# Seven block products for the gate projection in two more token groups, with the work beside them placed anew

## The chip, the cores and the metric

The kernel runs on one core of a Trainium2 chip. The metric is the device time of one execution in microseconds. An execution of the kernel before takes 316.2 to 318.2 us in 27 fast runs (median 316.66 in the last session), so a difference under about 0.5 us is read from the profiles, not from the times. All runs shown here were in the fast state.

In lines of the profile, PE is TensorE and PEld its weight loads, DVE is VectorE, ACT is ScalarE, POOL is GpSimd and SP is SyncE; POOL and SP issue the DMAs spoken of here. L593 is line 593 of that run's kernel, so line numbers differ between the kernel before and the changed one. A bank is one of the eight parts of PSUM, in which TensorE adds up its results.

## The reference, cut to what matters

```python
def _attn_ref(q, k, v):                      # 8 batches, 8 heads, 576 positions, 64 features
    q_p, k_p = phi(q, cos, sin), phi(k, cos, sin)     # phi(x) = [relu(x)*cos, relu(x)*sin]
    kv  = einsum('bhsf,bhsd->bhfd', k_p, v);  z = sum(k_p, axis=2)
    num = einsum('bhsf,bhfd->bhsd', q_p, kv)
    den = einsum('bhsf,bhf->bhs', q_p, z) + 1e-06
    return num / den

def _moe_ref(x, w_gate, w_val, w_out):       # x: 4608 tokens x 512;  d_ff = 1536
    g = x @ w_gate
    return (g * sigmoid(g) * (x @ w_val)) @ w_out
```

## The kernel before

The 4608 tokens go through in nine groups (0 to 8) of 512. A group has a **gate stage** (gate and value projections, twelve blocks of 128 features, one slot each) and an **output stage** (four slots). While TensorE works on group g, the attention of the tokens of group g+1 is done in gaps: `at(slot, function)` puts a piece of it after a slot. Sixteen slots make one group. A batch has 576 positions, so batches and groups don't coincide: from batch 4 on, the q of batch b is prepared while TensorE works on group b-2, so that of batch 7 in group 5.

In groups 7 and 8 the gate projection is formed from seven block products in place of eight, with additions between them on VectorE and copies on ScalarE:

```python
GATE = (7, 8)
...
rel  = ctx.enter_context(tc.tile_pool(name="rel", bufs=1))     # r_q: the weighted q of one batch
rawq = ctx.enter_context(tc.tile_pool(name="rawq", bufs=3))
...
def product(to, u, a, x, first):                               # one block product: 4 matmuls of 256 columns
    for i in range(2):
        for c in range(KH):
            nc.tensor.matmul(out=to[:, i], lhsT=a[:, c, 2 * u + i], rhs=x[:, :, c], ...)

for u in range(3):
    a = bank("a", fills=True);  product(a, u, A11, B11, True)
    b = bank("b", seeded=True); nc.scalar.copy(out=b, in_=a)
    e = bank("e", fills=True);  product(e, u, W3, X3, True)
    nc.scalar.copy(out=m7, in_=e); free("e")
    V(...)                                                      # a value block: 4 matmuls of 512 columns
    product(b, u, W2, X2, False)
    c = bank("c", seeded=True)
    nc.vector.tensor_tensor(out=c, in0=m7, in1=b, op=ALU.add)   # the seeding addition
    product(a, u, A12, B21, False); silu(u, 1, 0, a); free("a")
    if u: mul(u - 1, 1, 1)
    ...
    product(c, u, A22, X4, False)                               # needs the seeding addition
```

An attention tile takes two PSUM banks and is normalised on VectorE at once. A batch's q is weighted into `r_q` on VectorE (`phi_q`) and turned by a transposing DMA on SP's queue (`qturn_dma`, L306 before, L323 after) into `phit`, which the tiles read:

```python
def a_tile2(t):
    ps = take(2)
    ... nc.tensor.matmul(out=ps[...], lhsT=phit[b][...], rhs=kv2s[b % 2][...]) ...
    x_of(t, ps)                                # den, reciprocal, product: three VectorE instructions

def load_behind(b):                            # POOL
    nc.gpsimd.tensor_copy(out=hold2, in_=phit[b - 1][0:1, :, 0, 0, 0])     # waits until phit[b-1] has landed
    load(b, "q")
    if b > 3: load_kv(b)
```

In the output stage `product` runs through the two halves outermost, and the stores of `out` are issued on SP's queue, the same on which the turns are issued.

## Time and profile before

| kernel before | |
|---|---|
| median time | 316.97 us (3 runs), 316.86 us with the three of the next session |
| span of the profiled run | 314.5 us |
| TensorE busy | 307.5 us, 98% |
| length of groups 2 to 7 (first gate matmul to the next group's) | 32.62, 32.40, 32.74, 32.39, 32.43, 30.87 us |

The lines that carry the reading are in the prediction below. The group lengths are read from TensorE's timeline: the start of a group's first gate matmul, taken from the start of the next group's. They are the tool of this study, because they repeat from run to run within a few hundredths of a microsecond, except where a DMA decides.

### The profile page before, as it was taken

Reading aid. Unit: us, or ns where it says so; the run is one execution under the profiler, and the core shown is the slowest. Engines: PE = TensorE matmul, PEld = TensorE weight load, DVE = VectorE, ACT = ScalarE, POOL = GpSimd, SP = SyncE. Lnnn points to the kernel's source line nnn. Section 1 sums busy time; section 2 is a strip of 40 time slices with the busy share of each in tenths; the row PEclk is TensorE's granted clock in tenths of the full one; section 3 lists DMA queues with packets and bytes.
Section 4 is the critical chain, followed back from the end, with each engine's and each line's share of the span. In section 5 each row is a group of like instructions: output and inputs, shape, how many; then the busy total and the mean of one; then the engine's idle time right before and its main releaser. Section 6 shows DMA issues by size and latency. Waiting matters only on the chain.

```text
span 314.5 us, 6775 instructions
## 1 busy us (share of the span) xinstructions
PE 307.5 (98%) x2696; PEld 189.7 (60%) x2696; DVE 228.2 (73%) x458; ACT 143.4 (46%) x264; POOL 36.0 (11%) x62
## 2 busy tenths in 40 slices
PE   8899999999999999999999999999999999999994
PEld 4597455455444585548654764577456866687673
DVE  7873777697678888587748786778779478946772
ACT  7554545763335346334543454335533345324530
POOL 7855102000200200030003000300000000000000
PEclk9999999999999999999999999999999999999999
DMA  7999999996897994989495979598951160014004
GB/s 268 217 198 197 206 205 138 226 133 99 143 208 114 150 145 110 148 119 196 100 153 75 200 144 154 73 192 135 164 86 35 40 145 17 20 38 98 0 2 133
DMA packets 74767, 41.07 MB, mean 131 GB/s; under 512 B 49904, under 2 KB 69872, under 8 KB 74736
## 3 DMA queue, kind: packets, MB, share of 16 engines
q1 hardware_dynamic: 51952, 22.55, 38.0%
q0 software_dynamic: 22192, 17.57, 37.2%
q10 hardware_dynamic: 592, 0.52, 0.5%
q8 instruction: 21, 0.34, 0.4%
q14 instruction: 10, 0.08, 0.1%
HBM read 37.75 MB, written 9.44 MB: 150 GB/s over the span
## 4 chain that ended last, share of the span: by engine, by line
PE 91%; DVE 5%; ACT 2%; issue 1%; ACTq 0%
PE banks L564 46%; PE banks L786 20%; PE banks L729 6%; PE banks L633 5%; PE banks L621 5%; PE banks L333 3%; PE banks L448 3%; DVE ht L638 1%; PE banks L494 1%; PE banks L430 1%; DVE v L287 1%; DVE sums L760 1%; DVE x L471 1%; PE banks L197 1%; PE banks L536 0%
## 5 line engine op out<-in xcount | busy, mean ns | idle before, releaser
L564 PE MATMUL banks<-xT,wg_sb 128*128 128x512 f16 (+2 forms) x368 | 86.6, 360 | 0.0
L564 PE MATMUL banks<-xT,wv_sb 128*128 128x512 f16 (+2 forms) x368 | 86.6, 360 | 0.0
L570 ACT ACTIVATE sg<-banks 128x512 bf16<-128x512 f32 (+2 forms) x92 | 51.5, 560 | 76.0 <-PE banks L564 74.0
L575 DVE TENSOR_TENSOR ht<-sg,banks 128x512 f16<-128x512 bf16 (+2 forms) x92 | 57.9, 637 | 29.7 <-PE banks L564 22.7
L564 PEld LDWEIGHTS <-wv_sb 128*128 128x128 f16 x368 | 35.5, 98 | 37.4
L564 PEld LDWEIGHTS <-wg_sb 128*128 128x128 f16 x368 | 33.9, 98 | 31.5 <-issue 0.2
L786 PEld LDWEIGHTS <-ht 128*128 128x128 f16 x336 | 32.5, 98 | 4.2
L786 PEld LDWEIGHTS <-sums 128*128 128x128 f16 x252 | 24.5, 98 | 4.2 <-issue 0.8
L633 PE MATMUL banks<-xT,wv_sb 128*128 128x512 f16 x96 | 24.3, 379 | 0.0
L283 DVE TENSOR_TENSOR r_q<-raw_q,tab 128x1152 bf16<-128x1152 bf16 x24 | 17.6, 754 | 7.4 <-ACT raw_q L266 7.1
L729 PE MATMUL banks<-wo_sb,ht 128*128 128x512 f16 x96 | 22.7, 379 | 0.0
L471 DVE TENSOR_TENSOR x<-banks,rec 128x512 f16<-128x512 f32 (+1 forms) x32 | 21.6, 674 | 1.3 <-PE banks L430 0.3
L786 PE MATMUL banks<-wo_sb,ht 128*128 128x256 f16 x168 | 20.6, 273 | 0.0
L287 DVE TENSOR_TENSOR v<-raw_v,tab 128x1152 bf16<-128x1152 bf16 x27 | 19.9, 751 | 0.5 <-ACT raw_v L849 0.5
L786 PE MATMUL banks<-wt_sb,sums 128*128 128x256 f16 x168 | 19.8, 273 | 0.1
L786 PE MATMUL banks<-wt_sb,ht 128*128 128x256 f16 x168 | 19.5, 273 | 0.0
L799 ACT ACTIVATE ob<-banks 128x512 f32<-128x512 f32 x14 | 8.4, 597 | 21.9 <-PE banks L786 21.9
L638 DVE TENSOR_TENSOR ht<-sg,banks 128x512 f16<-128x512 bf16 x24 | 15.5, 681 | 2.4 <-ACT sg L627 2.4
L266 ACT ACTIVATE raw_k<-raw_k 128x576 bf16<-128x576 bf16 (+1 forms) x25 | 17.1, 694 | 0.0
L998 POOL COPY hold<-phit 1x2 bf16<-1x2 bf16 x5 | 1.4, 287 | 129.3 <-DMA phit<-r_q 129.3
L760 DVE TENSOR_TENSOR sums<-ht 128x1024 f16<-128x1024 f16 (+1 forms) x28 | 15.5, 553 | 0.4
L266 ACT ACTIVATE raw_q<-raw_q 128x576 bf16<-128x576 bf16 x24 | 15.4, 675 | 0.0
(121 smaller groups left out, 334.6 us busy)
## 6 DMA issues: line engine op xcount, KB each, us to landing
out_dram<-ob SPq DMA_DIRECT2D x67, 128.0 KB, 2.5
raw_k<-in_k_dram POOLq DMA_DIRECT2D x7, 576.0 KB, 8.8
raw_q<-in_q_dram POOLq DMA_DIRECT2D x6, 576.0 KB, 6.0
raw_v<-in_v_dram POOLq DMA_DIRECT2D x6, 576.0 KB, 11.4
wo_sb<-in_moe_w_out_dram POOLq DMA_DIRECT2D x3, 512.0 KB, 12.8
wg_sb<-in_moe_w_gate_dram POOLq DMA_DIRECT2D x5, 256.0 KB, 9.4
wv_sb<-in_moe_w_val_dram POOLq DMA_DIRECT2D x5, 256.0 KB, 9.5
wo_sb<-in_v_dram SPq DMA_DIRECT2D x2, 576.0 KB, 4.0
```

Of the source, the lines that this page charges most:

```text
L266: nc.scalar.activation(out=out, in_=in_, func=AF.Relu)
L283: nc.vector.tensor_tensor(out=st[b, "q"][:, g], in0=o.unsqueeze(2).to_broadcast([P, NC, 2, D]), in1=tab, op=ALU.mult)
L287: nc.vector.tensor_tensor(out=v2s[b == 1][:, g, :, :, 0:D], in0=(first if b == 0 and g == 0 else {"v": raw_of(b, "v")})["v"][:, g].unsquee ...
L471: nc.vector.tensor_tensor(out=st["x", t].rearrange("p (y e d) -> p e y d", e=2, d=D)[:, :, ys], in0=ps[:, :, 0:2 * J * D1].rearrange("p e ...
L564: nc.tensor.matmul(out=st["f", tg, fc, lo][i], lhsT=(wg_sb, wv_sb)[i][:, kc, fs], rhs=xT[tg][:, ts, kc], start=(kc == 0), stop=(kc == KC - 1))
L570: nc.scalar.activation(out=sg[:, 0:n], in_=st["f", tg, fc, lo][0], func=AF.Silu, scale=DOWN)
L575: nc.vector.tensor_tensor(out=ht[:, fc, r:r + n], in0=st.pop(("s", tg, fc, lo))[:, 0:n], in1=ps[1], op=ALU.mult)
L633: nc.tensor.matmul(out=val[u, i, w], lhsT=wv_sb[:, kc, fc * P:(fc + 1) * P], rhs=xT[tg][:, :, kc], start=(kc == 0), stop=(kc == KC - 1))
L638: nc.vector.tensor_tensor(out=ht[:, fc], in0=gates[u, w][:, i], in1=val.pop((u, i, w)), op=ALU.mult)
L729: nc.tensor.matmul(out=o_ps[t], lhsT=ht[:, fc, r:r + P], rhs=wo_sb[:, fc], start=(fc == 0), stop=(fc == FC - 1))
L760: nc.vector.tensor_tensor(out=o[:, lo:hi], in0=x[:, lo:hi], in1=y[:, lo:hi], op=op)
L786: nc.tensor.matmul(out=to[i][:, 0] if len(to) == 2 else to[0][:, i], lhsT=a[:, kc, i * P:(i + 1) * P], rhs=b[:, kc], start=first and kc == ...
```

## The change

The intent is to use the seven products in groups 5 and 6 also, which frees 1.2 us of TensorE in each, and to make room on VectorE and in PSUM so that nothing waits. The core of the diff:

```diff
-    GATE = (7, 8)
+    GATE = (5, 6, 7, 8)
+    AHEAD = 5
+    WSUM = (31, 39, 47, 63)
+    ROW = {... 5: ((8, 9, 12, 12), 13, (13, 13, 14, 15), 5),        # q weighting, turn, v products, kv slot
+           6: ((6, 8, 9, 12), 13, (13, 13, 14, 15), 3),
+           7: ([4 + i // 2 for i in range(18)], 13, (12, 13, 14, 15), 3)}
+    TILES = {... 5: (2, 4, 7, 9), 6: (0, 2, 5, 7), 7: (0, 1, 5, 7), 8: (0, 3, 5, 7)}
+    LATE = dict(M=44, V=87, O=131, X=26, x=150, ...)                # estimated ends of use, for the bank choice
...
-                bs = [min((b for b in free ...), key=lambda b: (not any(...), used[b]))]
+                bs = [min((b for b in free ...), key=lambda b: used[b])]
...
+    def phi_q_part(b, c, w):                    # batch 7: eighteen pieces on ScalarE
...
+        nc.scalar.activation(out=st[b, "q"][:, :, c, w], in_=raws[b, "q"][:, :, c], func=AF.Relu,
+                             scale=csk[:, c, w:w + 1])
...
-        x_of(t, ps)
+        if later:
+            behind.append(lambda: (x_of(t, ps), give_back(("a2", t), LATE["x"]), x_turn(t)))
+        else:
+            x_of(t, ps)
...
             nc.vector.tensor_tensor(out=c, in0=m7, in1=b, op=ALU.add)
+            while behind:
+                behind.pop(0)()
...
-            for i in range(2):
-                for kc in range(HC):
+            for kc in range(HC):
+                for i in range(2):
                     nc.tensor.matmul(out=to[i][:, 0] if len(to) == 2 else to[0][:, i], ...)
...
+        queues = (nc.gpsimd, nc.gpsimd) if tg > 0 else None          # stores of groups 1 to 7
...
         nc.gpsimd.tensor_copy(out=hold2, in_=phit[b - 1][0:1, :, 0, 0, 0])
-        load(b, "q")
+        if b < AHEAD:
+            load(b, "q")
         if b > 3:
             load_kv(b)
+        if AHEAD <= b + 1 < B:
+            load(b + 1, "q")
```

Cut: half of the kv evacuation is postponed in the same way, a gate product and token sums change places, and the slot arithmetic that `ROW` and `TILES` replace.

More of the change, by code (lines that the diff above doesn't have):

```diff
@@ L51 @@
     KH = KC // 2
-    GATE = (7, 8)
+    GATE = (5, 6, 7, 8)
+    AHEAD = 5
+    WSUM = (31, 39, 47, 63)
+    ROW = {2: ((16, 16, 17, 17), 18, (20, 21, 21, 22), 8), 3: ((12, 13, 14, 15), 18, (20, 20, 21, 21), 7),
+           4: ((12, 12, 13, 14), 15, (15, 16, 17, 18), 5), 5: ((8, 9, 12, 12), 13, (13, 13, 14, 15), 5),
+           6: ((6, 8, 9, 12), 13, (13, 13, 14, 15), 3), 7: ([4 + i // 2 for i in range(18)], 13, (12, 13, 14, 15), 3)}
+    TILES = {2: (0, 9, 10, 11), 3: (5, 9, 10, 11), 4: (5, 7, 9, 11), 5: (2, 4, 7, 9), 6: (0, 2, 5, 7), 7: (0, 1, 5, 7), 8: (0, 3, 5, 7)}
+    LATE = dict(M=44, V=87, O=131, X=26, x=150, v=(190, 250, 120, 150), e=130, a=90, c=170, b=110, k=120)
     consts = ctx.enter_context(tc.tile_pool(name="consts", bufs=1))
@@ L77 @@
     loose = [False]
+    rows = [0]
     def take(n, hold=None, fills=False, seeded=False):
@@ L84, in take @@
             if n == 1:
-                bs = [min((b for b in free if filled[b] or not seeded), key=lambda b: (
-                    not any(x != b and x + 1 != b and x + 1 in free for x in free), used[b]))]
+                bs = [min((b for b in free if filled[b] or not seeded), key=lambda b: used[b])]
             else:
@@ L105, in take, with touch, give_back @@
         return banks[:, b0] if n == 1 else banks[:, b0:b0 + n]
-    def touch(r):
+    def touch(r, late=1):
         now[0] += 1
+        if loose[0]:
+            for x in r:
+                used[x] = rows[0] + late
+            return
         for x in r:
             used[x] = now[0]
-    def give_back(hold):
-        touch(held.pop(hold))
+    def give_back(hold, late=1):
+        touch(held.pop(hold), late)
     raws = {}
@@ L284, in phi_q @@
                                 in1=tab, op=ALU.mult)
+    def phi_q_part(b, c, w):
+        if (b, "q") not in st:
+            st[b, "q"] = rel.tile([P, G, NC, 2, D], BF16, name="r_q")
+        nc.scalar.activation(out=st[b, "q"][:, :, c, w], in_=raws[b, "q"][:, :, c], func=AF.Relu,
+                             scale=csk[:, c, w:w + 1])
     def vmul(b, g):
@@ L347, in kv_out @@
                     in_=ps[hs, e, js.start * 2 * D1:js.stop * 2 * D1].rearrange("p (y x) -> p y x", x=D1))
+    behind = []
     kv2s = [consts.tile([P, 2, J, 2, D1], BF16, name=f"kv2_{j}") for j in range(2)]
@@ L353, in kv_out2, with part @@
         ps = st[b, "kvps"][:, :, 0:4 * J * D1 // 2].rearrange("p e (j w x) -> p e j w x", j=J, w=2)
-        for w, eng in enumerate((nc.scalar.copy, nc.vector.tensor_copy)):
+        def part(w, eng):
             for i in range(2):
                 eng(out=kv2s[b % 2][w * D:(w + 1) * D, :, :, i], in_=ps[i * D:(i + 1) * D, :, :, w])
+        part(0, nc.scalar.copy)
+        if b - 1 in GATE:
+            behind.append(lambda: (part(1, nc.vector.tensor_copy), kv_free(b)))
+        else:
+            part(1, nc.vector.tensor_copy)
     def kv_free(b):
-        give_back(("kv", b))
+        give_back(("kv", b), LATE["k"])
     def kv_first(j, lo=0, hi=NC):
@@ L435, in a_tile, with a_tile2 @@
                 )
-    def a_tile2(t):
+    def a_tile2(t, later=False):
         (b0, c0), (b1, c1) = (divmod(2 * t + r, NC) for r in range(2))
-        ps = take(2)
+        ps = take(2, ("a2", t))
+        rows[0] += LATE["X"]
         if b0 == b1:
@@ L452, in a_tile2 @@
                     )
-        x_of(t, ps)
+        if later:
+            behind.append(lambda: (x_of(t, ps), give_back(("a2", t), LATE["x"]), x_turn(t)))
+        else:
+            x_of(t, ps)
+            give_back(("a2", t), LATE["x"])
     def x_den(t, ps, ys=slice(0, 4)):
@@ L613, in bank, with free @@
             return take(1, ("g", tg, nm), **kw).rearrange("p (i x) -> p i x", i=2)
-        def free(nm):
-            give_back(("g", tg, nm))
+        def free(nm, late):
+            give_back(("g", tg, nm), late)
         def product(to, u, a, x, first):
+            rows[0] += LATE["M"]
             for i in range(2):
@@ L631, in V @@
             val[u, i, w] = take(1, ("v", tg, fc), fills=True)
+            rows[0] += LATE["V"]
             for kc in range(KC):
@@ L638, in mul @@
             nc.vector.tensor_tensor(out=ht[:, fc], in0=gates[u, w][:, i], in1=val.pop((u, i, w)), op=ALU.mult)
-            give_back(("v", tg, fc))
+            give_back(("v", tg, fc), LATE["v"][2 * w + i])
         def done():
@@ L653, in ffn_by_quarters @@
             nc.scalar.copy(out=m7, in_=e)
-            free("e")
+            free("e", LATE["e"])
             V(*((u - 1, 1, 1) if u else (u, 0, 0)))
@@ L659, in ffn_by_quarters @@
             nc.vector.tensor_tensor(out=c, in0=m7, in1=b, op=ALU.add)
+            while behind:
+                behind.pop(0)()
             product(a, u, A12, B21, False)
             silu(u, 1, 0, a)
-            free("a")
-            if u:
-                mul(u - 1, 1, 1)
+            free("a", LATE["a"])
             V(u, 0, 0) if u else V(u, 1, 0)
@@ L668, in ffn_by_quarters @@
             nc.vector.tensor_tensor(out=m7, in0=m7, in1=b, op=ALU.add)
+            while behind:
+                behind.pop(0)()
             silu(u, 0, 1, m7)
+            if u:
+                mul(u - 1, 1, 1)
             product(c, u, A22, X4, False)
             silu(u, 0, 0, c)
-            free("c")
+            free("c", LATE["c"])
             V(u, 1, 0) if u else V(u, 0, 1)
@@ L675, in ffn_by_quarters @@
             if u == 2:
-                for n in (1, 2):
-                    token_sum(n, 0, 4)
+                token_sum(1, 0, 4)
             mul(u, 0, 0)
@@ L683, in ffn_by_quarters @@
             silu(u, 1, 1, b)
-            free("b")
+            free("b", LATE["b"])
             if u:
@@ L687, in ffn_by_quarters @@
             mul(u, 0, 1)
+            if u == 2:
+                token_sum(2, 0, 4)
             if u:
                 done()
-                token_sum(*((3, 0, 4) if u == 1 else (4, 0, 4)))
+            if u == 1:
+                token_sum(3, 0, 4)
         V(2, 1, 1)
@@ L720, in store_two, with ffn_out @@
                 in_=obs[t // 2][e * SH:(e + 1) * SH, :, cols])
-    def ffn_out(t, f0=0, f1=None):
+    def ffn_out(t, f0=0, f1=None, queues=None):
         f1 = FC if f1 is None else f1
@@ L738, in ffn_out @@
             nc.vector.tensor_single_scalar(out=ob_of(t), in_=ps, scalar=DOWN, op=ALU.mult)
-        store(t)
+        store(t, queues=queues)
     aq = ht.rearrange("p (i w) (h t) -> p w h i t", w=2, h=2)
@@ L783, in product @@
         def product(to, a, b, first):
-            for i in range(2):
-                for kc in range(HC):
+            rows[0] += LATE["O"]
+            for kc in range(HC):
+                for i in range(2):
                     nc.tensor.matmul(out=to[i][:, 0] if len(to) == 2 else to[0][:, i],
@@ L816, in out_by_quarters @@
             nc.vector.scalar_tensor_tensor(out=o_, in0=x_, scalar=UP, in1=p_, op0=ALU.mult, op1=ALU.add)
-        token_sum(4, 4, 6)
+        token_sum(4, 0 if tg in GATE else 4, 6)
         slot_of(0)
@@ L836, in out_by_quarters @@
             for t in (t0 + 2, t0 + 3):
-                store(t)
+                store(t, queues=queues)
         slot_of(2)
@@ L842, in out_by_quarters @@
         for t in (t0, t0 + 1):
-            store(t, *((slice(HD, d_model), (nc.sync, nc.scalar)) if last else ()))
+            store(t, *((slice(HD, d_model), (nc.sync, nc.scalar)) if last else (slice(0, d_model), queues)))
         slot_of(3)
@@ L1013 @@
     for n in range(4):
-        at(SLOTS * (1 + n * (GATE[0] - 1) // 4) + FC + 3, lambda n=n: gate_weight_sum(n))
+        at(WSUM[n], lambda n=n: gate_weight_sum(n))
     for tg in GATE:
@@ L1019 @@
         s0 = SLOTS * (b - 1)
+        p0 = s0 - SLOTS
         keng = "dve" if b == 2 else "act"
-        steps = [lambda b=b, g=g: phi_q(b, g) for g in range(G)]
-        steps += [lambda b=b, g=g: (relu_k(b, g, g + 1, keng), vmul(b, g)) for g in range(G)]
-        if b == 2:
-            fs, tq = [s0 + i for i in (0, 0, 1, 1, 4, 5, 5, 6)], (s0 + 2, s0 + 2)
-        else:
-            p0 = s0 - SLOTS
-            fs, tq = [p0 + 12, p0 + 12] + [p0 + 11 + i for i in range(2, 8)], (p0 + 15, p0 + 16)
-            if b == 3:
-                fs, tq = [p0 + 12 + i for i in range(4)] + [s0 + 4, s0 + 4, s0 + 5, s0 + 5], (s0 + 2, s0 + 2)
-            at(p0 + 3 if b < 5 else p0 + 1, lambda b=b: load_behind(b))
@@ L1031 @@
-        tk = (s0 + 4, s0 + {2: 8, 3: 7}.get(b, 5))
-        for s, f in zip(fs, steps):
-            at(s, f)
-        for e in range(2):
-            at(tq[e], lambda b=b, e=e: qturn_dma(b, e))
-        at(tk[-1], lambda b=b: kv_mm(b), lambda b=b: kv_out2(b))
-        at(tk[-1] + 1, lambda b=b: kv_free(b))
-    for t in range(2 * OUT, NTG * OUT):
-        tg, i = divmod(t, OUT)
-        s = SLOTS * (tg - 1) + (5 if tg > 2 else 4) + 2 * i
-        if t == 2 * OUT:
-            at(s, a_(t, 0))
-            at(s + 1, a_(t, 1), turn(t))
-        elif tg == 2:
-            at((9, 10, 11)[i - 1] + SLOTS, lambda t=t: a_tile2(t), turn(t))
-            if i == 2:
-                at(11 + SLOTS, load_3)
-        else:
-            if t in (13, 14, 15):
-                s = SLOTS * 2 + t - 4
-            elif tg - 1 in GATE:
-                s = SLOTS * (tg - 1) + ((1, 2, 7, 9) if tg < 6 else (1, 2, 4, 7) if tg < 8 else (1, 2, 5, 6))[i]
-            at(s, lambda t=t: a_tile2(t), turn(t))
+        phi, turned, weighed, kv_slot = ROW[b]
@@ new lines @@
+        if b > 2:
+            at(p0 + (3 if b < 5 else 1), lambda b=b: load_behind(b))
+        if len(phi) > G:
+            for i, s in enumerate(phi):
+                at(p0 + s, lambda b=b, i=i: phi_q_part(b, *divmod(i, 2)))
+        else:
+            for g, s in enumerate(phi):
+                at(p0 + s, lambda b=b, g=g: phi_q(b, g))
+        for g, s in enumerate(weighed):
+            at(p0 + s, lambda b=b, g=g: (relu_k(b, g, g + 1, keng), vmul(b, g)))
+        for e in range(2):
+            at(p0 + turned, lambda b=b, e=e: qturn_dma(b, e))
@@ new lines @@
+        at(s0 + kv_slot, lambda b=b: kv_mm(b), lambda b=b: kv_out2(b))
+        if b - 1 not in GATE:
+            at(s0 + kv_slot + 1, lambda b=b: kv_free(b))
+    at(SLOTS + 4, a_(8, 0))
+    at(SLOTS + 5, a_(8, 1), turn(8))
+    for tg in range(2, NTG):
+        for i in range(tg == 2, OUT):
+            t, s = tg * OUT + i, TILES[tg][i]
+            later = tg - 1 in GATE and s in (0, 1, 3, 4, 7, 8)
+            at(SLOTS * (tg - 1) + s, lambda t=t, later=later: (a_tile2(t, later), None if later else x_turn(t)))
+            if t == 10:
+                at(SLOTS * (tg - 1) + s, load_3)
@@ L1056 @@
         if tg in GATE:
-            loose[0] = True
+            if not loose[0]:
+                loose[0] = True
+                rows[0] = max(used) + 1
             ffn_by_quarters(tg, lambda i: slot(s0 + i))
@@ L1067 @@
         for i in range(OUT):
-            ffn_out(tg * OUT + i)
+            ffn_out(tg * OUT + i, queues=(nc.gpsimd, nc.gpsimd))
             weight_sum(i)
```

## The prediction

> **What bounds the kernel now.** I read the page's busy shares first, then the chain of waits, then a table of busy time by stage, then the groups of instructions by shape.
>
> The page of the kernel before, busy time and the chain that ended last by engine:
> ```profile
> PE 307.5 (98%) x2696; PEld 189.7 (60%) x2696; DVE 228.2 (73%) x458; ACT 143.4 (46%) x264; POOL 36.0 (11%) x62
> ...
> PE 91%; DVE 5%; ACT 2%; issue 1%; ACTq 0%
> ```
> The reader is to see that TensorE is nearly always occupied and carries 91% of the chain. So there are two sources of gain: fewer columns streamed by TensorE, and its stalls. The median time is 316.97 us over a span of 314.5 us; I keep these 2.5 us as a constant.
>
> Busy time by stretch, in order group 6 whole, group 7's gate stage, its output stage, group 8's gate stage and its output stage (columns: stretch, length, PE busy, weight loads, DVE, ACT, POOL, clock, DMA share, GB/s):
> ```profile
> 217.83:250.26 32.43, 32.43 (x295) 19.69 (x293) 23.13 (x45) 12.27 (x22) 0.00 (x0) 1.00 0.49 86
> ...
> 250.26:271.71 21.45, 21.02 (x167) 13.93 (x165) 17.59 (x35) 9.90 (x18) 0.00 (x0) 1.00 0.34 75
> 271.71:281.13 9.42, 9.34 (x86) 8.14 (x85) 5.36 (x11) 2.36 (x4) 0.00 (x0) 1.00 0.00 1
> 281.13:300.66 19.53, 19.53 (x134) 12.91 (x133) 13.81 (x23) 9.76 (x18) 0.00 (x0) 1.00 0.24 55
> 300.66:310.01 9.35, 9.31 (x84) 7.87 (x82) 5.35 (x13) 2.42 (x5) 0.00 (x0) 1.00 0.19 48
> ```
> Groups 7 and 8 already form the gate by seven block products. Group 8's gate stage takes 19.53 us and group 7's 21.45 us. Group 7 alone also does four attention tiles, 0.26 us each in the chain: 1.04 us. The other 21.45 - 19.53 - 1.04 = **0.88 us is stall**. The chain names where:
> ```profile
> 255.73 0.27 PE banks L448 x8
> 256.02 0.18 DVE den L458
> 256.22 0.21 DVE rec L467
> 256.46 0.70 DVE x L471
> 257.20 0.60 PE banks L621 x4
> ...
> 263.70 0.35 PE banks L448 x8
> 264.07 1.28 DVE ht L638 x2
> 265.46 0.21 DVE rec L467
> 265.70 0.63 DVE x L471
> 266.33 0.57 issue
> 266.91 0.70 DVE banks L659
> 267.65 0.61 PE banks L621 x4
> ```
> The reader is to see an attention tile (L448) followed at once by its normalisation on VectorE (L458, L467, L471), and TensorE's next block product (L621) starting only after that: once because the tile's PSUM bank is handed to the next product, once because the addition that seeds a block's accumulator (L659) stands behind that normalisation in VectorE's order.
>
> The rows by shape that I take durations from:
> ```profile
> L564 PE MATMUL banks<-xT,wg_sb 128*128 128x512 f16 x312 | 80.1, 379 | 0.0
> ...
> L471 DVE TENSOR_TENSOR x<-banks,rec 128x512 f16<-128x512 f32 x30 | 20.7, 691 | 1.0
> ...
> L283 DVE TENSOR_TENSOR r_q<-raw_q,tab 128x1152 bf16<-128x1152 bf16 x24 | 17.6, 754 | 7.4 <-ACT raw_q L266 7.1
> ...
> L266 ACT ACTIVATE raw_q<-raw_q 128x576 bf16<-128x576 bf16 x24 | 15.4, 675 | 0.0
> ```
> A matmul's 379 ns is latency; its rate comes from the chain: eight of 512 columns in 1.73 us there (0.216 each), eight of 256 in 0.87 us (0.109 each).
>
> **What the Trainium skill says.** "TensorE: Matmul & The Clock Gate", Wait — 56ns, not 53.3ns?: a warm matmul takes N / 2.4 GHz plus about 2.5 ns, so 215.7 ns at 512 columns and an estimated 109.2 ns at 256. The trace agrees (0.216 and 0.109), so halving the width costs almost nothing. "VectorE: DVE Perf Modes", The TRN2 errata: an fp32 addition takes (N+151)/0.96 ns, 691 ns at 512; the trace has 695 for L659 and 686 for L668. "ScalarE: Activation LUTs", What ACT_TABLE_LOAD costs: 186 ns + 0.833 ns per element, 93 ns more for a per-partition scale, neighbours overlapping by 93 ns. For the new 256-element pieces I estimate 186 + 213 + 93 = 492 ns, 0.4 us back to back; L504, of 260 elements with such a scale, shows 475. "SBUF — State Buffer", Who interferes with whom: DMA does not contend with compute engines, but descriptors written by GpSimd can be held up by VectorE. That matters for the moved stores; no trace yet shows it.
>
> **The change part by part.**
> 1. Gate of groups 5 and 6 by seven products. Before: 12 blocks x 4 = 48 matmuls of 512 columns, 48 x 0.216 = 10.37 us a group. After: 3 x 7 x 4 = 84 of 256, 84 x 0.109 = 9.14 us. Saved 1.22 us, twice: **-2.44 us**, all on the path, as TensorE is the path there. The instruction order confirms 72 more matmuls.
> 2. Its price on VectorE: four differences of 0.42 (1.67), three additions of 0.695 and three of 0.686 (4.14): 5.8 us a group; on ScalarE six copies of 0.58 (3.5 us). None of it is on the path unless VectorE becomes late. In issue order group 5 then has, on VectorE: 12 gate products 8.2, four tiles 4.2, block additions 4.1, token sums 4.3, three output additions 2.1, four v products 3.0, kv copies 0.9, differences 1.7: 28.4 us. Neighbours overlap: in the group before, a like sum of 26.7 shows as 24.7 busy, a factor 0.93. So about 26.3 us against some 31.2 us of TensorE; group 6, without the v products, 23.6. In the gate stage alone about 19 of 21.8. Tight, not bound.
> 3. Room made for it: batch 7's query weighting goes from VectorE (4 x 0.754 = 3.0 us less) to ScalarE (18 x about 0.45 = 8 us, less the four dropped 0.675: about +5.4 us, to some 22 of 31 us in group 5); batches 5 and 6 are turned earlier, inside the gate stage; attention tiles move to earlier slots. Net 0 on the path.
> 4. Tile normalisations and half of the kv evacuation wait until after the seeding addition, a last gate product moves behind the m7 addition, and a token sum leaves its place ahead of them. PSUM banks go by estimated end of use instead of by last touch. Both aim at group 7's 0.88 us. I give back two thirds: **-0.6 us**.
> 5. Chunks outermost in the output stage: the four chunks whose sums are early come first for both halves, so the last sums have 4 x 0.109 = 0.44 us more. The chain shows gaps of 0.03 us in seven output stages and about 0.07 in group 7: **-0.2 us**.
> 6. Weight sums sooner: the same four 0.95 us instructions, elsewhere: 0. Stores of groups 1 to 7 go through POOL instead of SP: 56 issues of about 0.75 us are 42 us of an engine that is busy 36 of 314; 0 on the path.
> 7. New stalls in groups 5 and 6, which do what group 7 does plus kv (and, in group 5, v) work: by the same reasoning 0.88 x 1/3 = 0.3, plus 0.05 for the kv copies: **+0.7 us** for both.
>
> Sum: -2.44 - 0.6 - 0.2 + 0.7 = about -2.6 us: 316.97 - 2.6 = **314.4 us**, -0.8%.
>
> **The rivals.**
> VectorE becomes the bound in groups 5 and 6. For it: the last third of their gate stage issues 8.5 us on VectorE (7.9 after overlap), while TensorE has seven products of 0.435, four value blocks of 0.864 and a tile of 0.26, 6.8 us in all; so VectorE ends it about 1 us late. Against: the token sums at its end are needed only some 3 us into the output stage, where VectorE has 5.4 of 9.4 us of work. If it comes true, each group loses about 1 us more: 316.4 us.
> PSUM banks become the wait. For it: at the kv slot a pair for kv, a pair for a tile whose evacuation is now postponed, three or four accumulators and one or two value banks fill all eight. The postponed reading that protects the seeding addition keeps a pair longer. Against: the new choice hands out the bank that ends soonest. It would cost 0.3 to 0.7 us per group: 315 to 316 us.
> The stores on POOL hold back loads, or wait for a load's guard there. For it: POOL waited 129 us for query turns before. Against: that wait is idleness, an output buffer is needed again only a group (31 us) later, and DMA stores land in 2.5 us in the trace. If false, a late load would show as several us, above 317.
> Everything fits: no new stalls and all of group 7's recovered: -2.44 - 0.88 - 0.2, 313.4 us. TensorE's own work allows little below that, so faster by over 2% (below 310.6) would need savings that I cannot find.
>
> **Range and chances.** From the ceiling of 313.4 with some 0.6 for unseen small gains, to a VectorE-bound result with something lost: 312.8 to 316.6 holds eight in ten. Over 2% faster: 0.02; within 2%: 0.96; slower by over 2%: 0.02.
>
> **What would show each step.** Part 1: 168 matmuls of 256 columns in groups 5 and 6 in place of 96 of 512, at 0.109 us, and a period per group down from 32.5 to about 31.3 to 31.7 us. Part 4: group 7's gate stage at 20.6 to 21.0 us, without the normalisation between L448 and a block product in the chain. Part 5: output stages of 9.3 us without the 0.03 us break. Part 7: VectorE's share of the chain in groups 5 and 6 under 1 us. I am wrong if those groups stay at 32.4 us (VectorE or banks took the gain), or if groups 1 to 4 change length, on which I count for nothing.

## The result, and the profile after

The changed kernel takes 315.99 us (median of 6 runs, 315.36 to 316.55) against 316.86 us (6 runs). The ratio is 0.997, 95% interval 0.9951 to 0.9989. Ratios are computed as the mean time of one kernel's fast runs over that of the other's fast runs of the same rounds, so they are not quite the ratio of the medians quoted. The gain is 0.3%, or 0.9 us, where the prediction had 0.8% and 2.6 us. The time itself lies inside the stated range, 312.8 to 316.6 us.

The page of the changed kernel, the same two lines as before:
```profile
PE 303.5 (97%) x2768; PEld 196.8 (63%) x2768; DVE 235.3 (75%) x470; ACT 153.6 (49%) x290; POOL 65.5 (21%) x118
...
PE 78%; DMA 13%; DVE 4%; POOL 1%; issue 1%; ACT 1%; DVEq 0%
```
TensorE is busy for 4.0 us less, but it is idle for 3.3 us more, so the span is only 0.7 us shorter. Most of DMA's 13% is weight loads at the start, which this chain happens to follow there; group 1 starts only 0.11 us later.

The table by stretch: group 5, group 6, then group 7's gate and output stage and group 8's gate stage (columns as in the prediction):
```profile
186.50:219.41 32.91, 31.56 (x322) 23.38 (x321) 26.49 (x50) 22.27 (x47) 5.90 (x12) 1.00 0.88 129
...
219.41:250.64 31.23, 31.23 (x330) 23.13 (x329) 24.37 (x47) 13.45 (x25) 4.19 (x9) 1.00 0.37 72
250.64:271.20 20.56, 20.56 (x167) 13.93 (x165) 16.90 (x34) 9.87 (x18) 3.77 (x8) 1.00 0.32 77
271.20:280.37 9.17, 9.17 (x87) 8.22 (x85) 5.80 (x11) 2.36 (x4) 0.38 (x1) 1.00 0.01 3
280.37:299.90 19.53, 19.53 (x135) 12.92 (x133) 13.23 (x22) 9.75 (x18) 3.77 (x8) 1.00 0.20 55
```
In group 6 the block products save all they can: 31.23 us, of which TensorE is busy 31.23. Group 7's gate stage falls from 21.45 to 20.56 us, so all of its 0.88 us of stall is gone. Only group 5 is not full: 32.91 us, of which 31.56 busy.

| group | before | after | difference | predicted |
|---|---|---|---|---|
| 2 | 32.62 | 33.37 | +0.75 | 0 |
| 3 | 32.40 | 32.88 | +0.48 | 0 |
| 4 | 32.74 | 32.46 | -0.28 | 0 |
| 5 | 32.39 | 32.91 | +0.52 | -0.87 |
| 6 | 32.43 | 31.23 | -1.20 | -0.87 |
| 7 | 30.87 | 29.73 | -1.14 | -0.67 |

Group 8, to the start of its last output product, is 0.14 us shorter and the start of group 1 is 0.11 us later. With these the differences sum to -0.90 us, which is how much earlier that product starts (308.5 and 307.6 us). "Predicted" spreads the terms of the prediction's sum over the groups: -1.22 + 0.35 in groups 5 and 6, -0.6 - 0.07 in 7; what is left of part 5, about 0.1 us, lies in the other groups. So the gain was larger than predicted where it was expected, except in group 5. Against the prediction, groups 2, 3 and 5 lost 2.6 us (0.75 + 0.48 + 1.39).

TensorE's timeline of the changed kernel, the two places where groups 2 and 3 lose (in brackets idle time before the row and what ended it):
```profile
121.00 1.02 PE L593 MATMUL banks<-xT,wg_sb 128*128 128x512 f16 x4 [0.58 <-DMA xT<-x]
...
152.58 1.47 PE L825 MATMUL banks<-wo_sb,sums 128*128 128x256 f16 x12 [0.53 <-DVE ob L866]
```
The first gate matmul of group 3 waits for a tile's turn by DMA; the last output product of group 3 waits for VectorE's addition L866, which reads the same bank. VectorE's timeline shows what stands ahead of L866, two weightings (L294) and two v products (L304):
```profile
149.16 1.42 DVE L294 TENSOR_TENSOR r_q<-raw_q,tab 128x1152 bf16<-128x1152 bf16 x2
150.50 1.42 DVE L304 TENSOR_TENSOR v<-raw_v,tab 128x1152 bf16<-128x1152 bf16 x2
151.84 0.69 DVE L866 SCALAR_TENSOR_TENSOR ob<-banks,ob 128x512 f32<-128x512 f32 x1
```

The chain of waits in group 5, and ScalarE's and POOL's timeline at the same time:
```profile
201.62 0.89 PE banks L651 x8
202.54 0.58 ACT sg L657
203.12 0.80 ACT r_q L300 x2
203.91 0.49 ACT banks L680
204.44 1.03 PE banks L651 x8
```
```profile
199.93 0.91 ACT L300 ACTIVATE r_q<-raw_q,cs_all 128x256 bf16<-128x256 bf16 x2 [1.83 <-DMA xT<-x]
...
199.93 0.17 POOL L1037 COPY hold<-phit 1x2 bf16<-1x2 bf16 x1 [9.64 <-DMA phit<-r_q]
```
ScalarE's first weighting piece (L300) starts at 199.93 us after 1.83 us of idleness. Behind it stand the gate's activation (L657) and the copy that seeds a block (L680), and TensorE waits for that. The profile names "DMA xT" as the releaser, but POOL's guard, which waits for `phit` of batch 6 and for nothing else, is released at the same 199.93 us. L300 writes `r_q`, of which there is one buffer; it can be written when batch 6's turn has read it.

**The theory** was therefore: the parts entered as "0 on the path" cost. (a) In group 5, batch 7's pieces wait for the single `r_q` buffer. (b) In group 2, the additional load of batch 5's q on POOL delays a tile's turn. (c) In group 3, batch 5's weighting and v products overfill VectorE. **Rivals**: ScalarE's additional work itself; POOL's stores slowing all turns; and losses that only move when one is mended.

### The profile page after: what moved, and what is told of

Same layout as the page of the kernel before. It is cut to its first block, busy times and chain, and to the rows that moved or that the text cites. A ratio compares the mean times of both kernels' runs of the same rounds, so it can differ in the third digit from the quotient of the medians.

```text
span 313.8 us, 6938 instructions
## 1 busy us (share of the span) xinstructions
PE 303.5 (97%) x2768; PEld 196.8 (63%) x2768; DVE 235.3 (75%) x470; ACT 153.6 (49%) x290; POOL 65.5 (21%) x118
## 4 chain that ended last, share of the span: by engine, by line
PE 78%; DMA 13%; DVE 4%; POOL 1%; issue 1%; ACT 1%; DVEq 0%
PE banks L593 26%; PE banks L825 16%; PE banks L664 13%; PE banks L651 11%; PE banks L766 7%; DMA wv_sb<-in_moe_w_val_dram 4%; DMA wo_sb<-in_moe_w_out_dram 4%; DMA wg_sb<-in_moe_w_gate_dram 3%; PE banks L350 2%; DMA xT<-x 2%; PE banks L473 2%; DMA wo_sb<-in_v_dram 1%; PE banks L523 1%; DVE sums L797 1%; DVE ht L604 1%
## 5 line engine op out<-in xcount | busy, mean ns | idle before, releaser
L599 ACT ACTIVATE sg<-banks 128x512 bf16<-128x512 f32 (+2 forms) x68 | 37.2, 547 | 53.8 <-PE banks L593 49.6
L593 PE MATMUL banks<-xT,wg_sb 128*128 128x512 f16 (+2 forms) x272 | 62.0, 354 | 0.6 <-DMA xT<-x 0.6
L593 PE MATMUL banks<-xT,wv_sb 128*128 128x512 f16 (+2 forms) x272 | 62.0, 354 | 0.0
L604 DVE TENSOR_TENSOR ht<-sg,banks 128x512 f16<-128x512 bf16 (+2 forms) x68 | 41.6, 622 | 23.4 <-PE banks L593 16.0
L748 POOL DMA_DIRECT2D out_dram<-ob x56 | 29.3, 532 | 121.8 <-ACT ob L838 117.1
L664 PE MATMUL banks<-xT,wv_sb 128*128 128x512 f16 x192 | 48.6, 379 | 0.0
L669 DVE TENSOR_TENSOR ht<-sg,banks 128x512 f16<-128x512 bf16 x48 | 31.1, 682 | 3.7 <-ACT sg L657 3.7
L657 ACT ACTIVATE sg<-banks 128x512 bf16<-128x512 f32 x36 | 20.5, 589 | 12.0 <-PE banks L651 12.0
L651 PEld LDWEIGHTS <-wgs_sb 128*128 128x128 f16 x192 | 17.8, 98 | 7.7 <-issue 0.9
L651 PE MATMUL banks<-kvt,wgs_sb 128*128 128x256 f16 x144 | 21.6, 273 | 0.6 <-DVE x L500 0.3
L304 DVE TENSOR_TENSOR v<-raw_v,tab 128x1152 bf16<-128x1152 bf16 x27 | 19.7, 753 | 0.5 <-ACT raw_v L888 0.5
```

What stands on the lines that cost most here:

```text
L304: nc.vector.tensor_tensor(out=v2s[b == 1][:, g, :, :, 0:D], in0=(first if b == 0 and g == 0 else {"v": raw_of(b, "v")})["v"][:, g].unsquee ...
L593: nc.tensor.matmul(out=st["f", tg, fc, lo][i], lhsT=(wg_sb, wv_sb)[i][:, kc, fs], rhs=xT[tg][:, ts, kc], start=(kc == 0), stop=(kc == KC - 1))
L599: nc.scalar.activation(out=sg[:, 0:n], in_=st["f", tg, fc, lo][0], func=AF.Silu, scale=DOWN)
L604: nc.vector.tensor_tensor(out=ht[:, fc, r:r + n], in0=st.pop(("s", tg, fc, lo))[:, 0:n], in1=ps[1], op=ALU.mult)
L657: nc.scalar.activation(out=gates[u, w][:, :, j * HT:(j + 1) * HT], in_=src, func=AF.Silu, scale=DOWN)
L664: nc.tensor.matmul(out=val[u, i, w], lhsT=wv_sb[:, kc, fc * P:(fc + 1) * P], rhs=xT[tg][:, :, kc], start=(kc == 0), stop=(kc == KC - 1))
```

## The experiments

All kernels gave correct results. Times are medians of fast runs; "before" was 316.6 to 316.7 us in each session. The group lengths of all profiled runs:

| kernel | 2 | 3 | 4 | 5 | 6 | 7 | time, ratio to before |
|---|---|---|---|---|---|---|---|
| before | 32.62 | 32.40 | 32.74 | 32.39 | 32.43 | 30.87 | |
| after | 33.37 | 32.88 | 32.46 | 32.91 | 31.23 | 29.73 | 315.99, 0.9970 |
| e1 pieces later | 33.23 | 32.89 | 32.45 | 31.91 | 31.24 | 29.73 | 314.72, 0.9931 |
| e2 q load later | 32.62 | 32.89 | 32.45 | 33.45 | 31.23 | 29.73 | 315.37, 0.9954 |
| e3 stores on SP | 34.36 | 32.88 | 32.45 | 31.92 | 31.23 | 29.79 | 314.40, 0.9925 |
| e4 weighting sooner | 33.50 | 32.97 | 32.45 | 33.03 | 31.23 | 29.73 | 315.89, 0.9972 |
| e5 turn 6 sooner | 33.36 | 32.89 | 32.59 | 31.92 | 31.24 | 29.72 | 314.71, 0.9936 |
| e6 gate alone | 32.61 | 32.40 | 32.62 | 36.50 | 33.91 | 30.75 | 321.47, 1.0152 |
| e7 no gate in 5, 6 | 34.09 | 32.89 | 32.44 | 33.27 | 32.43 | 30.26 | 318.16, 1.0050 |
| e8 not postponed | 33.20 | 32.89 | 32.45 | 33.05 | 32.48 | 31.27 | 318.31, 1.0050 |
| e9 halves outermost | 33.10 | 32.89 | 32.45 | 32.73 | 31.37 | 29.86 | 316.31, 0.9997 |
| e10 weighting back | 33.65 | 32.39 | 32.45 | 33.10 | 31.23 | 29.73 | 315.57, 0.9963 |
| e11 three undone | 32.62 | 32.96 | 33.50 | 31.92 | 31.24 | 29.73 | 315.44, 0.9967 |
| e12 mended | 32.62 | 32.70 | 32.46 | 31.93 | 31.24 | 29.73 | 313.92, 0.9921 |

**e1, batch 7's pieces two slots later.**
```diff
-           ... 7: ([4 + i // 2 for i in range(18)], 13, (12, 13, 14, 15), 3)}
+           ... 7: ([6 + i // 2 for i in range(18)], 15, (12, 13, 14, 15), 3)}
```


> The changed kernel with batch 7's eighteen ScalarE pieces two slots later (slots 6 to 14 instead of 4 to 12) and its turn at slot 15 instead of 13; ScalarE does the same work. Theory (the first piece waits for the single r_q buffer until batch 6's turn has landed, ScalarE falls behind and holds the block products' copies): group 5, now 32.91 us, falls to 31.2 to 31.8 us, the 1.8 us idle of ScalarE before L300 goes, total about 1.2 to 1.6 us less than the changed kernel. Rival (ScalarE's 8 us of additional work itself delays the copies): group 5 stays at 32.5 us or more.

ScalarE's timeline of this run has the first pieces without a wait:
```profile
201.19 0.89 ACT L300 ACTIVATE r_q<-raw_q,cs_all 128x256 bf16<-128x256 bf16 x2
```
Group 5 falls by 1.00 us to 31.91, just above the 31.2 to 31.8 us expected, with the same work on ScalarE, and the time by about 1.3 us. So the work itself is not what cost; the wait is. What is left over 31.2 us are two waits of 0.35 and 0.33 us, for a bank that a tile's normalisation still reads and at the kv products, for which the prediction had +0.35 in this group.

**e5, batch 6's turn sooner.** A second way to the same cause, from the other end.
```diff
-           ... 6: ((6, 8, 9, 12), 13, (13, 13, 14, 15), 3),
+           ... 6: ((4, 6, 8, 9), 10, (13, 13, 14, 15), 3),
```


> The changed kernel with batch 6's query weighting at slots 4, 6, 8, 9 of group 4 and its turn at slot 10 instead of 13; batch 7's ScalarE pieces stay where they are. A second way to the same cause as the run with later pieces. Theory (single r_q buffer, free only when batch 6's turn has landed): the turn lands at some 195 us instead of 199.9 us, ScalarE's 1.8 us idle before L300 goes, group 5 falls from 32.91 to about 31.9 us as with the later pieces. Rival (the later pieces helped only because their place suits ScalarE better): group 5 stays at 32.7 us or more.

Here the pieces have not moved, and they start without a wait, at 198.08 us:
```profile
198.08 0.89 ACT L300 ACTIVATE r_q<-raw_q,cs_all 128x256 bf16<-128x256 bf16 x2
```
The turn landed at 190.3 us, earlier still than the 195 us expected. Group 5 is 31.92 us. With e1 this shows cause (a): worth 1.0 us. A second `r_q` buffer would have been the plainest test, but it does not fit in SBUF (with `bufs=2` the program does not build, for want of space).

**e2, batch 5's q load later.** The load is put behind a guard that waits for group 2's last turn.
```diff
+    def load_q5():
+        nc.gpsimd.tensor_copy(out=hold2, in_=xT[3][0:1, 3, 0, 0:2])
+        load(AHEAD, "q")
+    at(SLOTS * 2 + FC, load_q5)
...
-        if AHEAD <= b + 1 < B:
+        if AHEAD < b + 1 < B:
```


> The changed kernel with the load of batch 5's q held back on POOL until the last x tile of group 2 is turned. Theory (this extra 576 KB load runs beside that turn and makes it land after TensorE is ready): group 2, now 33.21 us, back to 32.6 us; the 0.58 us wait of the gate matmul L593 for DMA xT goes. Rival (the stores moved to POOL, or chance, slow the turn): group 2 stays at 33.0 us or more.

TensorE's first gate matmul of group 3 has no wait in front any more:
```profile
120.24 1.03 PE L593 MATMUL banks<-xT,wg_sb 128*128 128x512 f16 x4
```
Group 2 is back at 32.62 us exactly. In the nine profiled runs that keep the early load (after, e1, e3, e4, e5, e7, e8, e9, e10) group 2 takes 33.1 to 34.4 us, always longer, by a different amount each time; in the five without it (before, e2, e6, e11, e12) it takes 32.6. That shows (b): 0.5 to 1.7 us, and it is the part of the changed kernel that varies. Group 5 was 0.5 us longer than in the changed kernel: all of it came earlier by 0.8 us, the turn landed only 0.2 us earlier (the first piece at 199.71 us), and the `r_q` wait grew from 1.83 to 2.38 us. So two losses were coupled, and mending one returned part of it to the other.

**e3, stores back on SP.**
```diff
-        queues = (nc.gpsimd, nc.gpsimd) if tg > 0 else None
+        queues = None
...
-            ffn_out(tg * OUT + i, queues=(nc.gpsimd, nc.gpsimd))
+            ffn_out(tg * OUT + i)
```


> The changed kernel with all output stores back on SP's queue. Theory (stores are not what costs; group 2's loss is the q load, group 3's is VectorE order, group 5's is the r_q buffer): groups 2 and 3 keep 33.2 and 33.0 us; in group 5 batch 6's turn goes behind eight stores, as in the kernel before, so it lands as late or later and the group stays at 32.9 us or more; total within 0.5 us of the changed kernel or slower. Rival (POOL's stores slow the turns): groups 2 and 5 each become 0.5 us or more shorter.

I had the order on SP wrong: with the turn at slot 13 it now stands ahead of the eight stores, not behind. Batch 6's turn released POOL's guard at 194.46 us (199.93 in the changed kernel), ScalarE's first piece started without a wait, and group 5 became 31.92 us, as the rival had it:
```profile
194.46 0.18 POOL L1037 COPY hold<-phit 1x2 bf16<-1x2 bf16 x1 [29.14 <-DMA phit<-r_q]
...
198.98 0.90 ACT L300 ACTIVATE r_q<-raw_q,cs_all 128x256 bf16<-128x256 bf16 x2
```
So moving the stores back takes away all of the 1.0 us of (a), as e1 and e5 do. That loss needed both moves of the change: pieces early enough to meet the turn, and stores beside the turn that made it late. A batch is turned in two halves, each a DMA of its own. The second half of batch 6's turn took 13.1 us from issue to landing in the changed kernel and 6.6 us here; the median over all halves is 8.0 us (13.1 at most) there and 6.5 us (8.4) here. Group 2 did not gain: in the profiled run it lost even 1.57 us to the same tile's turn, so there the stores on POOL are not the cause. The four times of this kernel spread from 313.7 to 315.5 us.

**e4 and e10, batch 5's weighting.** One place sooner, then back to where the kernel before had it.
```diff
 e4:
-           ... 5: ((8, 9, 12, 12), 13, (13, 13, 14, 15), 5),
+           ... 5: ((7, 8, 9, 12), 13, (13, 13, 14, 15), 5),
 e10:
+           ... 5: ((12, 12, 13, 14), 15, (15, 16, 17, 18), 5),
```


> The changed kernel with batch 5's four query weightings on VectorE at slots 7, 8, 9, 12 instead of 8, 9, 12, 12 of group 3, so that one instruction of 0.75 us fewer stands ahead of the output addition L866. Theory (VectorE's order makes L866 late and the last output product waits for it): group 3, now 33.05 us, goes to 32.4 to 32.6 us and the 0.53 us wait before the last twelve L825 matmuls goes. Rival (VectorE is simply full in group 3, so it only moves the wait): group 3 stays at 32.9 us or more.

TensorE's timeline of e4:
```profile
144.74 1.47 PE L825 MATMUL banks<-wo_sb,ht 128*128 128x256 f16 x12 [0.25 <-DVE x L500]
...
152.97 1.47 PE L825 MATMUL banks<-wo_sb,sums 128*128 128x256 f16 x12 [0.15 <-DVE ob L866]
```
This expectation failed: the wait at L866 shrank from 0.53 to 0.15 us, and 0.25 us appeared in front of the output stage. Group 3 did not get shorter. VectorE runs without a gap from 137 to 148 us there, so it matters little which of its instructions is the late one.

> The changed kernel with batch 5's weighting and turn where the kernel before had them (slots 12, 12, 13, 14, v products from slot 15 on). Theory (moving them into group 3's late slots is what fills VectorE there): group 3 from 32.88 to 32.4 us, group 4 unchanged within 0.2 us. Rival (group 3 is late through something else, such as the weight sum at its slots): group 3 stays at 32.8 us or more.

Group 3 is 32.39 us, as before the change, and group 4 stays. No v products stand ahead of L866 any more:
```profile
149.44 2.26 DVE L294 TENSOR_TENSOR r_q<-raw_q,tab 128x1152 bf16<-128x1152 bf16 x3
151.62 0.68 DVE L866 SCALAR_TENSOR_TENSOR ob<-banks,ob 128x512 f32<-128x512 f32 x1
```
That shows (c): 0.49 us, for having put two weightings into the late half of group 3's gate stage, and v products ahead of L866. The run undoes both at once, so which of the two costs it is not shown. The gain does not show fully in the times (315.57 us, 17 runs from 314.19 to 316.41), because group 2 varies: 33.65 us in this profile.

**e6, the block products alone.** The kernel before with one line changed.
```diff
-    GATE = (7, 8)
+    GATE = (5, 6, 7, 8)
```


> The kernel before with block products also in groups 5 and 6 and nothing else of the change. Theory (block products save 1.22 us a group, but without the rest of the change stalls as in group 7 return it): groups 5 and 6 at 31.5 to 32.4 us each against 32.4, group 7 still at 30.9 us, groups 2 to 4 as before within 0.1 us, total 0 to 1.8 us under the kernel before. Rival (the room made in groups 2 to 5 is needed; without it VectorE is the bound): groups 5 and 6 at 32.8 us or more, total above the kernel before.

The time is 321.47 us, 1.5% slower than before: the rival was right, and the loss went further than it said. TensorE's timeline at the start of group 5:
```profile
186.70 0.60 PE L621 MATMUL banks<-kvt,wgs_sb 128*128 128x256 f16 x4 [0.77 <-DVE kvt L605]
...
189.51 0.61 PE L621 MATMUL banks<-kvt,wgs_sb 128*128 128x256 f16 x4 [1.35 <-DVE kvt L605]
```
The block products need differences of the turned tokens (L605), so here a group's tiles would have to be turned before its first slot, not during it. VectorE waited 2.25 us for the turn and TensorE for VectorE. So the first waits come from a late turn, where the rival had a full VectorE. Groups 5 and 6 lose 4.1 and 1.5 us; the two waits shown are 2.1 of this, and the rest was not taken apart. The room that the change makes is needed.

**e7, the block products of groups 5 and 6 taken out.** `GATE` also switches the postponement and the new bank choice, so in groups 5 and 6 these go too.
```diff
-    GATE = (5, 6, 7, 8)
+    GATE = (7, 8)
```


> The changed kernel with block products only in groups 7 and 8, as in the kernel before; everything else of the change kept. Theory (block products are worth 1.22 us a group on TensorE; group 5's loss is due to the r_q wait): group 6 at 32.3 to 32.6 us instead of 31.23, group 5 at 32.4 to 33.0, groups 2 and 3 still 33.2 and 32.9, groups 7 and 8 as changed; total 316.5 to 317.5, at or above the kernel before. Rival (the gain of group 6 comes from placement and not from fewer columns): group 6 at 31.7 us or less.

Group 6 is 32.43 us with eight products and 31.23 with seven: 1.20 us, against 1.22 predicted. The time is 318.16 us, a microsecond over what I expected; group 2 was slow (34.09 us), group 5 at 33.27 lost more to the `r_q` wait than I had thought (ScalarE idles 3.57 us there), and group 7 is 30.26 us where 29.73 was expected; why is not shown. What is left of the change costs 1.5 us over the kernel before; the two groups bring 2.2 us back.

**e8, tiles normalised at once.**
```diff
-            later = tg - 1 in GATE and s in (0, 1, 3, 4, 7, 8)
+            later = False
```


> The changed kernel with attention tiles normalised at once and not after the seeding addition; bank choice and order of sums as changed. Theory (the postponement is what recovered group 7): group 7 from 29.73 to 30.2 to 30.7 us, groups 5 and 6 0.3 to 0.8 us longer each. Rival (the bank choice recovered it): group 7 at 29.9 us or less.

TensorE's timeline, the largest of the new waits:
```profile
228.24 1.24 PE L350 MATMUL banks<-v,raw_k 64*64 64x130 bf16 x72 [0.79 <-DVE ht L669]
...
260.19 0.42 PE L473 MATMUL banks<-kv,phit 128*128 128x65 bf16 x8 [0.43 <-DVE ht L669]
```
Group 7 takes 31.27 us, more than in the kernel before, and group 6 32.48; the kernel is slower than before (1.0050). Postponing is worth 1.54 us in group 7, 1.25 in group 6 and only 0.14 in group 5, which loses elsewhere. In group 7 that is more than the 0.88 us of stall that the postponement was to remove. The bank choice's estimates count on it, which may be why; this is not shown. The bank choice by itself was not tried.

**e9, halves outermost in the output stage.**
```diff
-            for kc in range(HC):
-                for i in range(2):
+            for i in range(2):
+                for kc in range(HC):
```


> The changed kernel with the output stage's halves outermost again, as in the kernel before. Theory (chunks outermost gives the late sums 0.44 us): the break of 0.03 us before the last product returns, groups 5 to 7 0.1 to 0.3 us longer in the output stage, total 0.2 to 0.8 us above the changed kernel. Rival (the order is worth nothing): group lengths as changed within 0.05 us.

Groups 6, 7 and 8 are each 0.13 to 0.14 us longer, groups 3 and 4 the same, and group 5 even 0.18 us shorter: its gate stage gained 0.40 us, as the `r_q` wait was shorter by chance (1.43 us), and its output stage lost 0.22. So the order is worth about 0.6 us in the output stages of groups 5 to 8, and nothing in groups 3 and 4. The 20 times run from 315.07 to 319.52 us, so the total alone would not have shown it.

**e11 and e12, combinations.** e11 undoes three moves: stores (as e3), q load (as e2), weighting (as e10). e12 leaves the stores on POOL and takes e1, e2 and e10 together.

> The changed kernel with three of its moves undone: stores on SP, the load of batch 5's q behind group 2's last turn, batch 5's weighting as in the kernel before. Theory (these three cost what the prediction missed): group 2 at 32.6, group 3 at 32.4, group 5 at 31.9, groups 6 to 8 as in the changed kernel; total some 2.3 us under the changed kernel, 313.6 us, 1.0% under the kernel before. Rival (the losses only move on, as when the sooner weighting moved the wait): 315 us or more.

TensorE's timeline of e11:
```profile
153.50 1.04 PE L593 MATMUL banks<-xT,wg_sb 128*128 128x512 f16 x4 [0.40 <-DMA xT<-x]
...
170.35 0.32 PE L473 MATMUL banks<-kv,phit 128*64 128x65 bf16 x7 [0.79 <-DMA phit<-r_q]
```
Groups 2 and 5 gained, but with the weighting and turn late again and the stores on the same queue, batch 5's turn stood behind eight stores and the tile in group 4 waited for it: group 4 at 33.50 us. Group 3 did not gain either (32.96 us), as group 4's first gate matmul waited 0.40 us for a tile's turn. The losses had moved on, and the rival was right: 315.44 us. The stores and the q load alone, without moving the weighting back, were not tried together.

> The changed kernel with three repairs, stores left on POOL: batch 5's q load behind group 2's last turn, batch 5's weighting and turn as in the kernel before, batch 7's ScalarE pieces two slots later. Theory (the three losses are separate and each repair holds): groups 2 to 5 at 32.6, 32.4, 32.5, 31.9 us, groups 6 to 8 as in the changed kernel, total 313.5 to 314.0 us, 0.9% under the kernel before. Rival (losses move on, as with stores on SP, where batch 5's turn came late for group 4's tile): one of groups 3 to 5 at 0.5 us above these, total 314.5 us or more.

313.92 us, 0.9921 of the kernel before (95% interval 0.9903 to 0.9939), and faster than both kernels. It is not shown to be faster than e3 or e1 alone, whose intervals (0.9899 to 0.9951, 0.9916 to 0.9946) overlap with it. TensorE waits 0.35 and 0.33 us in group 5, and nowhere else in groups 2 to 8 does the timeline name a wait. But group 3 is 32.70 us, 0.3 above e10, with a gap before group 4:
```profile
153.23 1.04 PE L593 MATMUL banks<-xT,wg_sb 128*128 128x512 f16 x4
```
The timeline does not name its releaser, but the trace has the last tile's turn landing at 153.18 us, 6.9 us after its issue, beside the load of batch 6's q (140.9 to 152.6 us). In e10 that load ended at 148.8 us and the turn took 2.8 us. In e12 the loads started later, because the turn of batch 4, which releases them, landed at 138.7 us against 134.1. So part of group 2's loss seems to have moved into group 3, as in e11; no run tests this.

## Why the prediction was wrong

**The bound** was read rightly: TensorE, with its stalls and its columns as the two sources of gain. Two slips change little. The constant of 2.5 us pairs a median with the span of a faster run; run by run the time is 1.7 to 1.8 us over the span, and it drops out of the difference. And the terms sum to -2.54 us, rounded there to -2.6.

**Part 1** (-1.22 us a group) was right: 1.20 in group 6, measured against e7. **Part 2** (VectorE tight, not bound) was right: VectorE is busy for 26.5 us in group 5, where 26.3 was worked out. **Part 7** had +0.7 us for both groups: 0.68 us of waits remain in group 5 and none in group 6, so the sum is right by luck, as its even spread was not. The VectorE rival did not come true in groups 5 and 6, but VectorE held TensorE up in group 3, where I had not looked. **Part 4** was too small: I counted on two thirds of 0.88 us, and all of it came back. e8 shows that it needs the postponement; e7 suggests that this is not enough, as group 7 kept its own there and its gate stage took 21.09 us, not 20.56. **Part 5** had 0.2; e9 shows about 0.6, in four output stages and not in eight.

**The steps that failed** are part 3, "Net 0 on the path", part 6, "0 on the path", and a move that has no term in the sum:
- "batch 7's query weighting goes from VectorE ... to ScalarE": I had counted ScalarE's 22 of 31 us, which was right (22.27), and a piece took 500 ns, against 492 estimated. I had not asked what the first piece waits for. In the kernel before the same buffer was written twelve slots after the turn (slot 16 of group 4, then slot 12 of group 5), so the single buffer never showed; now it is seven slots (13, then 4), and that costs 1.0 us (e1, e5). The prediction read ScalarE's load, and the cost was a release.
- "batches 5 and 6 are turned earlier, inside the gate stage": for batch 5 this costs 0.49 us (e10). I had worked out VectorE's sum for groups 5 and 6 and not for groups 3 and 4, into which work was moved.
- Part 6, the stores on POOL: TensorE's timeline names no wait for a load, which the third rival had feared, and POOL was busy for only 21% of the span. But stores on another queue ran beside the turn of batch 6, and it took 13.1 us and not 6.6 (e3). This is the same 1.0 us as in the first point and not another: taking back either move removes it.
- The load of the next batch's q (`AHEAD`), which the sum doesn't mention at all: it runs beside the last turns of group 2 and costs 0.5 to 1.7 us (e2).

In numbers: these give back 1.0 + 0.5 + about 0.75 = 2.25 us in the profiled run. Groups 4, 6 and 7 did better than predicted by 0.28 + 0.33 + 0.47 = 1.08. The rest of 2.6 - 0.9 = 1.7 us missing is the second of group 5's two bank waits (0.33) and the small differences in groups 1 and 8. The prediction did say that it would be wrong if groups 1 to 4 changed length; that is where about half of the shortfall lies.

## What to carry to other kernels

Where work is moved to make room, ask of each moved instruction what releases it at its new place, which buffer it overwrites and who read that last; busy shares don't show it. Work out the load of the stages that receive work as carefully as of those that are relieved. And measure by stage: the total moved by 0.9 us, while stages moved by -1.2 to +0.75, and repairs of one loss lengthened another (group 5 in e2, group 4 in e11, group 3 in e12), so repairs have to be tried together.

## What the Trainium skill lacked or had wrong

- "DMA: Bandwidth & Descriptors", Anatomy of one DMA, fits a DMA issued from GpSimd as 2.0 us plus bytes over 436 GB/s; for a store of 128 KB that is an estimated 2.3 us. Here the 56 stores on POOL had a median of 4.9 us from issue to landing, many of them beside turns and loads; on SP in the kernel before it was 2.5 us. What made the difference was not separated. The fit is for a DMA by itself; what that section lacks is a time for one that has others beside it.
- In the pages that I looked up, none says how long a transposing DMA takes beside ordinary ones. Here half a batch's turn took 6.6 us to land (median, 8.5 at most) with the stores on its own queue in the kernel before, and 8.0 us (13.1 at most) with them on POOL's in the changed one.
